# Loading the last 64 rows of w1 onto both partition halves, in a fused LayerNorm, scan and MLP kernel

## The chip, the cores and the metric

The kernel runs on one core of one Trainium2 chip. The metric is the device time of one launch in microseconds: 144.88 us, the median of three runs (144.66 to 145.1). A profile of one more execution gives every instruction's start and duration on the five engines: TensorE (PE, its weight loads as PEld), VectorE (DVE), ScalarE (ACT), GpSimd (POOL) and the queue engine SyncE (SP), which issues most DMAs.

## What is computed

All inputs are bf16; x has 2048 tokens of width D = 448, the MLP is F = 1792 wide. Cut to what matters:

```
xn = layernorm(x)                                   # over the 448 features
# branch A: diagonal complex scan over 2048 tokens
Bu[t] = B_bar @ xn[t];  h[t] = Lam_bar * h[t-1] + Bu[t]
s[t]  = 2 * Re(C @ h[t]) + xn[t] * Dskip
# branch B: LayerNorm again, then the MLP
y = layernorm(xn);  hdn = gelu(y @ w1 + b1);  g = silu(hdn @ w2 + b2)
out = x + s * g
```

## The kernel before

**Groups.** The tokens are worked in four groups g = 0 to 3 of 512, each made of two blocks b of 256 consecutive tokens. A block's even and odd tokens (`par` 0 and 1) stand side by side on 128 partitions, so each group has four tiles of 128 tokens.

**LayerNorm.** `ln_stats` and `ln_scale` give two scale and offset pairs per token: one for xn (branch A, tile `xn_sb`) and one for the doubly normalised y (branch B, tile `xn2_sb`). `ln_apply` (lines 444 to 453) writes 448 normalised columns into a row of 512. The last 64 columns are needed twice, since the rows are then transposed in pieces of 128 and every matmul uses 64 rows of the array at a time. For xn, `tail_twice` copies the last 64 columns behind themselves. For y, `ln_apply` writes two parts: columns 0 to 383, and then columns 320 to 447 (so the fourth piece of 128 begins with columns 320 to 383, which also stand in the third). A DMA transpose on SP (line 468) turns the rows into `xnT` or `xn2T`. The first block of group 0 is quicker: `first_stats` and `first_apply` (lines 384 to 422) work on each parity alone, and TensorE does the transposes of block 0 (line 415; pieces taken by `tcols`), which ACT and DVE then copy out of PSUM.

**The first MLP matmul, `mm1`.** `w1_sb` is 128 partitions by four row pieces by 1792 columns. Pieces 0 to 2 hold rows 0 to 383 of w1. Piece 3 holds rows 384 to 447 on partitions 64 to 127 (load `w1r`, line 348) and, on partitions 0 to 63, a copy of rows 320 to 383 that ACT or DVE makes from piece 2 after each load (line 342, keys `w1c_0` to `w1c_3`). `mm1_phase` (lines 655 to 675) computes a pair of F tiles (128 columns each, two PSUM banks) in two phases: the first does three row pieces, the second four, and within a step the two 64-row halves of the array work on two banks at once. After the second phase ACT does a Gelu per F tile into `gT`. For group 0 the two blocks are done apart (256 columns at a time), for the other groups 512 columns at a time. Every phase waits for its column chunk of w1 (`w1_0` to `w1_3`) and for `w1r`, a second phase for the copied rows too. w1 and w2 come in column chunks of 2, 4, 4 and 4 F tiles (`CH`, line 336).

**The rest.** `mm2` (and `mm2_tokens` for group 3) is the second MLP matmul, `bu_phase` is B_bar @ xn, `ssm` the scan on DVE, `yt` the output matmul of branch A. The tables for branch A (`parameters`, `tables`, `lb`, `cq`) are made on the chip from the small inputs; `b1_columns` turns b1 into columns by small matmuls from `brows`.

**The order of the work.** Every step is a task with the keys it reads and writes. `ORDER` (line 154) is a written-out list of task numbers; each engine and each DMA queue takes its own tasks in that order, and a task waits for the tasks whose keys it needs. `SECOND` lists the tasks that go to their second engine (ACT or DVE, POOL or DVE). SP takes, in this order: x block 0 even, odd, x block 1, `w1_0`, `w1r`, `w1_1`, `w1_2`, `w1_3`, the transpose of block 1, x blocks 2 and 3, four chunks of w2, the B matrices, and so on. The ACT queue takes seven small loads at the start: three vectors for branch A, b1 as three rows of 512 and one of 256, Dskip and b2. `dummies` are matmuls on constants whose result nobody reads.

Of the kernel before, what the change touches and what calls it, by code (L numbers as in the profile page):

```python
# [979 lines left out]
```

## Time and profile before

| what | value |
|---|---|
| time, median of three runs | 144.88 us (144.66 to 145.1) |
| the profiled execution | 145.18 us, of which the span from first to last instruction is 143.4 us |
| PE busy | 137.7 us, 96% of the span |
| DVE, ACT, POOL busy | 126.0, 105.9 and 24.7 us |
| DMA | 16.21 MB in 38530 packets |

A line of the timeline reads: start and duration in us, engine, code line, operation, tile written and tile read, shape, count, and in brackets the idle time ahead of it and what ended that. In a line of groups, the numbers behind the bar are busy us and the mean ns of one. L305 and L306 are the two arms of the helper `copy` (ACT and DVE), L77 and L78 the two forms of a DMA (transpose and plain), and L667 is every matmul of `mm1`. A line of DMA issues ends with the count, the KB of each and the median us from issue to landing. SPq and ACTq are the queues as issuers. The tables of windows give, for each stretch, the busy time of each engine, the granted TensorE clock, the share of busy DMA engines and the GB/s.

### The profile page before, as it was taken

The page shows a single profiled execution, that of the slowest core. Times are in us where ns is not written, and L with a number is a line of the kernel's source. Part 1 is how long each engine was busy: PE and PEld are TensorE (multiplying, and loading weights), DVE is VectorE, ACT ScalarE, POOL GpSimd, SP SyncE. Part 2 cuts the span into 40 slices and gives each one's busy share as a digit, 9 for nine tenths or more (in the row PEclk, how much of TensorE's full clock was granted, in tenths as well). Part 3 has the DMA queues.
Part 4 walks back from the last instruction along what each step waited for, and adds up shares of the span by engine and source line. Part 5 has one row for each costly group of instructions (what it writes and reads, how often), then busy time and mean ns, then how long its engine had stood idle before and what let it go on. Part 6 is the DMA issues. An engine that isn't in the chain of part 4 may idle for free.

```text
span 143.4 us, 3549 instructions
## 1 busy us (share of the span) xinstructions
PE 137.7 (96%) x1422; PEld 90.9 (63%) x1422; DVE 126.0 (88%) x275; ACT 105.9 (74%) x197; POOL 24.7 (17%) x83
## 2 busy tenths in 40 slices
PE   7999998999999989999999999999999999999991
PEld 7879953464455854566558844588777677665560
DVE  2979878998999679999999989993699998999994
ACT  3699959999996879879889359451777999928300
POOL 3389760256000700001000000200000001000000
DMA  4979997799997961010010745099830000003233
GB/s 101 240 238 249 311 331 184 152 245 184 199 189 148 151 134 35 0 32 0 7 32 0 61 108 110 0 199 193 160 126 9 0 5 0 18 5 69 49 119 128
DMA packets 38530, 16.21 MB, mean 113 GB/s; under 512 B 32937, under 2 KB 38066, under 8 KB 38514
## 3 DMA queue, kind: packets, MB, share of 16 engines
q1 hardware_dynamic: 38352, 15.92, 49.5%
q8 instruction: 11, 0.18, 0.5%
q10 hardware_dynamic: 162, 0.07, 0.2%
q14 instruction: 5, 0.04, 0.1%
HBM read 6.09 MB, written 1.84 MB: 55 GB/s over the span
## 4 chain that ended last, share of the span: by engine, by line
PE 63%; DMA 14%; DVE 13%; SPq 4%; ACT 1%; issue 1%; POOL 1%; DVEq 0%; ACTq 0%
PE psum L667 15%; PE psum L698 13%; PE psum L792 9%; PE psum L853 7%; DMA Bn<-in_A_B_re_dram 6%; PE psum L817 5%; DMA xnT<-xn_sb 5%; PE psum L816 5%; PE psum L382 3%; DMA Cr<-in_A_C_im_dram 3%; SPq L78 3%; DVE tmp L601 2%; DVE Bn L602 2%; PE psum L869 2%; PE psum L866 2%; DVE xn_sb L451 2%
## 5 line engine op out<-in xcount | busy, mean ns | idle before, releaser
L667 PE MATMUL psum<-xn2T,w_sb 64*128 64x512 bf16 (+1 forms) x490 | 46.5, 334 | 0.7 <-DMA w_sb<-in_B_w_dram 0.3
L673 ACT ACTIVATE gT<-psum,b1f 128x512 bf16<-128x512 f32 (+1 forms) x70 | 37.5, 607 | 4.5 <-PE psum L667 4.2
L667 PEld LDWEIGHTS psum<-xn2T,w_sb 64*128 64x128 bf16 x490 | 26.6, 108 | 13.9 <-ACT gT L673 1.0
L792 PE MATMUL psum<-gT,w_sb 128*128 128x512 bf16 x126 | 28.0, 379 | 0.7 <-ACT gT L673 0.6
L698 PE MATMUL psum<-xnT,BT 64*128 64x256 bf16 x392 | 25.0, 269 | 0.4 <-DVE u_sb L721 0.4
L698 PEld LDWEIGHTS psum<-xnT,BT 64*128 64x128 bf16 x392 | 19.2, 94 | 6.7 <-issue 1.0
L792 PEld LDWEIGHTS psum<-gT,w_sb 128*128 128x128 bf16 x126 | 11.9, 98 | 15.6 <-issue 1.5
L757 DVE TENSOR_TENSOR_SCAN s_w<-vs,dk 128x1048 f32<-128x1048 bf16 (+1 forms) x8 | 16.3, 2057 | 0.1
L452 ACT ACTIVATE xn_sb<-x_all,lnw 128x448 bf16<-128x448 bf16 (+2 forms) x16 | 10.0, 665 | 5.4 <-DMA xnT<-xn_sb 3.8
L853 PE MATMUL psum<-w_sb,gT 128*128 128x448 bf16 x56 | 10.9, 352 | 0.0
L474 ACT ACT_TABLE_LOAD x8 | 10.3, 1283 | 0.4
L305 ACT ACTIVATE ue<-psum 128x512 bf16<-128x512 f32 (+1 forms) x12 | 6.4, 562 | 5.3 <-PE psum L698 5.2
L451 DVE TENSOR_SCALAR xn_sb<-x_all,lnw 128x448 bf16<-128x448 bf16 (+2 forms) x24 | 8.0, 362 | 0.9 <-DVE lnw L441 0.5
L853 PEld LDWEIGHTS psum<-w_sb,gT 128*128 128x128 bf16 x56 | 5.5, 98 | 4.8 <-ACT psum L305 0.2
L305 ACT ACTIVATE vs<-s_w 64x258 bf16<-64x258 f32 (+2 forms) x11 | 6.5, 612 | 2.7 <-DVE s_w L757 2.6
L816 PE MATMUL psum<-hx,CZ 128*128 128x256 bf16 x63 | 8.4, 275 | 0.0
L817 PE MATMUL psum<-Bn,CQ 128*128 128x256 bf16 x63 | 8.2, 273 | 0.2 <-DVE Bn L777 0.2
L767 POOL TENSOR_TENSOR cur<-ang 128x8 f32<-128x8 f32 x2 | 0.4, 204 | 41.6 <-DVE ang L766 41.6
L798 ACT ACTIVATE g_sb<-psum,db 128x512 bf16<-128x512 f32 (+1 forms) x12 | 7.1, 629 | 0.6 <-PE psum L792 0.6
L369 DVE BATCH_NORM_STATS2 lnst<-x_all 128x6 f32<-128x448 bf16 x12 | 7.1, 613 | 0.4 <-DMA x_all<-in_A_x_dram 0.4
L816 PEld LDWEIGHTS psum<-hx,CZ 128*128 128x128 bf16 x63 | 5.9, 98 | 2.3 <-issue 0.4
L824 DVE TENSOR_TENSOR t<-psum,g_sb 128x512 bf16<-128x512 f32 (+1 forms) x12 | 7.1, 614 | 0.1
(161 smaller groups left out, 207.1 us busy)
## 6 DMA issues: line engine op xcount, KB each, us to landing
x_all<-in_A_x_dram SPq DMA_DIRECT2D x3, 448.0 KB, 4.3
w_sb<-in_B_w_dram SPq DMA_DIRECT2D x3, 448.0 KB, 5.3
out_dram<-Bn SPq DMA_DIRECT2D x6, 224.0 KB, 2.7
w_sb<-in_B_w_dram SPq DMA_DIRECT2D x3, 384.0 KB, 5.5
w_sb<-in_B_w_dram SPq DMA_DIRECT2D x2, 224.0 KB, 4.5
Bn<-in_A_B_im_dram SPq DMA_DIRECT2D x1, 336.0 KB, 6.5
Bn<-in_A_B_re_dram SPq DMA_DIRECT2D x1, 336.0 KB, 8.5
out_dram<-w_sb SPq DMA_DIRECT2D x3, 112.0 KB, 1.8
```

Of the source, the lines that this page charges most:

```text
L305: kb.either(("act", [lambda e, o=o, i=i: e.activation(o, i, ACT.Copy) for o, i in pairs]), ("dve", [lambda e, o=o, i=i: e.tensor_copy(o, i ...
L451: kb.either(("dve", [lambda e, o=o, i=i: e.tensor_scalar(o, i, rs, nb, op0=ALU.mult, op1=ALU.add) for o, i in parts]), ("act", [lambda e, ...
L452: ("act", [lambda e, o=o, i=i: e.activation(o, i, ACT.Identity, bias=nb, scale=rs) for o, i in parts]),
L474: kb.add("act", lambda e: e.preload_act_table_set(what), reads, writes, sem=name)
L667: return lambda e: e.matmul(dst(bk[k]), w1_sb[rows, d, fcol(2 * j + k)], rhs[rows, d], start=not second and n == 0, stop=second and n == 3)
L673: act(lambda e, k=k, fi=fi: e.activation(gT[:, gb, fi, cols], psum[:, bk[k], cols], ACT.Gelu_apprx_tanh, bias=b1f[:, fi:fi + 1]), ["b1f", ...
L698: fns.append(lambda e, rows=rows, bank=bank, m=m, o=o, n=n: e.matmul(psum[:, bank, c * NK:(c + 1) * NK].rearrange("p (b c) -> p b c", b=2) ...
L757: dve(lambda e, so=so, vi=vi, di=di: e.tensor_tensor_scan(so, vi, di, 0.0, ALU.add, ALU.mult), ["v", "vl", "vz", "dk", "dk01"] + ["v3"] * ...
L792: pe([lambda e, fi=fi: e.matmul(psum[:, bk, :], w2_sb[:, fi, 128 * j:128 * j + 128], gT[:, gb, fi, :], start=fi == 0, stop=fi == NF - 1) f ...
L816: pe([lambda e, k=k: e.matmul(par(psum[:, bk, :], 1), CZ[:, k, cols], halves(hx[:, hb, k, 1:NK + 1]), start=False, stop=k == 6, skip_group ...
L817: pe([lambda e, k=k: e.matmul(par(psum[:, bk, :], 0), CQ[:, k, cols], halves(hz[:, hb, k, :]), start=False, stop=k == 6, skip_group_check= ...
L853: pe([lambda e, fi=fi: e.matmul(P, gT[:, gb, fi, 128 * q:128 * q + 128], w2_sb[:, fi, :], start=False, stop=fi == NF - 1, skip_group_check ...
```

## The change

- `w1r` is now one DMA that writes all 128 partitions of piece 3: rows 384 to 447 of w1 twice, once onto each half. Its source pattern has a leading dimension of 2 with step 0. The copies of rows 320 to 383 (four tasks) are gone. Both halves of the array use piece n in step n, and a first phase no longer waits for `w1r`.
- The transposed y has the same form: `ln_apply` writes 448 columns in one part for both branches, and a new `tail` (the former `tail_twice`) doubles the last 64 columns, now for y too. TensorE's transposes of block 0 are three of 128 columns and two of 64 (`turn`).
- w1 and w2 come in chunks of 4, 4 and 6 F tiles.
- b1 is loaded as two rows of 512 and one of 768 and turned by ten small matmuls instead of six; Dskip and b2 are loaded from SP instead of ACT.
- In `parameters` one small operation is merged away, one ACT Exp over two columns becomes two, and one Abs may go to DVE. Four dummies are gone.
- `ORDER` and `SECOND` are new.

```diff
-            CH = ((0, 2), (2, 4), (6, 4), (10, 4))
+            CH = ((0, 4), (4, 4), (8, 6))
...
                 ld("sp", w1_sb[:, 0:3, a:a + w], dram_ap(B_w1, a, [[F, 128], [128 * F, 3], [1, w]]), [f"w1_{c}"])
-                copy([(w1_sb[0:64, 3, a:a + w], w1_sb[64:128, 2, a:a + w])], [f"w1_{c}"], [f"w1c_{c}"])
...
             ldx(1, 1)
+            ld("act", brows[0:2, 0:512], dram_ap(B_b1, 0, [[512, 2], [1, 512]]), ["br0"], ["br"])
+            ld("act", brows[2:3, :], dram_ap(B_b1, 1024, [[768, 1], [1, 768]]), ["br1"], ["br"])
             ldw1(0)
-            ld("sp", w1_sb[64:128, 3, :], dram_ap(B_w1, 384 * F, [[F, 64], [1, F]]), ["w1r"])
-            ld("act", brows[0:3, :], dram_ap(B_b1, 256, [[512, 3], [1, 512]]), ["br0"], ["br"])
-            ld("act", brows[3:4, 0:256], dram_ap(B_b1, 0, [[256, 1], [1, 256]]), ["br1"], ["br"])
-            for i, vec in enumerate((A_Dskip, B_b2)):
-                ld("act", drows[i:i + 1, :], dram_ap(vec, 0, [[D, 1], [1, D]]), [f"dbr{i}"])
+            ld("sp", w1_sb[:, 3, :], dram_ap(B_w1, 384 * F, [[0, 2], [F, 64], [1, F]]), ["w1r"])
             ldw1(1)
             ldw1(2)
-            ldw1(3)
+            for i, vec in enumerate((A_Dskip, B_b2)):
+                ld("sp", drows[i:i + 1, :], dram_ap(vec, 0, [[D, 1], [1, D]]), [f"dbr{i}"])
...
-            def tcols(b, par, d):
-                a = par * 512 + (0, 128, 256, 320)[d]
-                return xn2_sb[:, b, a:a + 128]
+            def turn(b, par, bank):
+                row, o = xn2_sb[:, b, par * 512:par * 512 + D], psh[:, bank, 0:512].rearrange("p (d c) -> p d c", d=4)
+                return [lambda e, d=d: e.transpose(o[:, d], row[:, 128 * d:128 * d + 128], ident[:, :]) for d in range(3)] \
+                    + [lambda e, h=h: e.transpose(o[h, 3], row[:, 384:D], ident[:, :]) for h in (slice(0, 64), slice(64, 128))]
...
+            def tail(rows, keys):
+                v = rows.rearrange("p b (r c) -> p (b r) c", r=2)
+                o, i = v[:, :, D:512], v[:, :, 384:D]
+                kb.either(("dve", lambda e: e.tensor_copy(o, i)), ("act", lambda e: e.activation(o, i, ACT.Copy)), keys, keys)
...
-                parts = [(row[:, 0:384], src[:, 0:384]), (row[:, 384:512], src[:, 320:D])] if which else [(row[:, 0:D], src)]
-                kb.either(("dve", [lambda e, o=o, i=i: e.tensor_scalar(o, i, rs, nb, op0=ALU.mult, op1=ALU.add) for o, i in parts]),
-                          ("act", [lambda e, o=o, i=i: e.activation(o, i, ACT.Identity, bias=nb, scale=rs) for o, i in parts]),
+                row = row[:, 0:D]
+                kb.either(("dve", lambda e: e.tensor_scalar(row, src, rs, nb, op0=ALU.mult, op1=ALU.add)),
+                          ("act", lambda e: e.activation(row, src, ACT.Identity, bias=nb, scale=rs)),
...
-                    rows, d = slice(64 * h, 64 * h + 64), (0, 1, 2 + h, 3 - h)[n]
+                    rows, d = slice(64 * h, 64 * h + 64), n
...
-                   xk2 + [f"w1_{c}", "w1r"] + ([f"w1c_{c}"] if second else []), [f"ps{bk[0]}", f"ps{bk[1]}"], split=True)
+                   xk2 + [f"w1_{c}"] + ["w1r"] * second, [f"ps{bk[0]}", f"ps{bk[1]}"], split=True)
...
-            dummies(4, ["st0"])
```

What the new order says, as far as the prediction speaks of it. SP: x block 0 even, odd, x block 1, `w1_0` (4 F tiles), `w1r`, `w1_1` (4), `w1_2` (6), the transpose of block 1, Dskip, x blocks 2 and 3, the first chunk of w2, b2, half of B, the other two chunks of w2, the other half of B, its two short ends, x blocks 4 and 5. PE: two first phases (both of chunk `w1_0`), two second phases (both of `w1_0`), and then chunk `w1_1`. DVE at the start: the stats of block 0, the apply of its even half, the first stats of block 1, two small steps, the apply of the odd half, a memset, the second stats of block 1 and two small steps, and then the copy of the odd half's transposes out of PSUM.

More of the change, by code (lines that the diff above doesn't have):

```diff
@@ L228, in bass_recurrent_scan__ssm_conv_s5__mixer_channel_mlp__prompt_kernel @@
         vrows = dk.bitcast(BF)[:, 1, 0:512]
-        brows = vrows[32:36, :]
+        brows = dk.bitcast(BF).rearrange("p i c -> p (i c)")[32:35, 2 * NS:2 * NS + 768]
         cw = SB("cw", [128, 32, 4], F32)
@@ L408, in first_apply @@
                     key = xk(0)[par:par + 1] if b == 0 else xk(1)
-                    parts = [(dst, src)] if b == 0 else [(xn2_sb[:, 1, par * 512:par * 512 + 384], src[:, 0:384]), (xn2_sb[:, 1, par * 512 + 384:par * 512 + 512], src[:, 320:D])]
-                    dve([lambda e, o=o, i=i, mean=mean, r1=r1: e.tensor_scalar(o, i, mean, r1, op0=ALU.subtract, op1=ALU.mult) for o, i in parts],
+                    dve(lambda e, dst=dst, src=src, mean=mean, r1=r1: e.tensor_scalar(dst, src, mean, r1, op0=ALU.subtract, op1=ALU.mult),
                         key + [f"r1{q}", f"mv0_{q}"], [f"xm{b}p{par}"])
@@ L414, in first_apply @@
                     bank, oap = 6 - par, xn2T[:, 0, b, par * 4:par * 4 + 4, :]
-                    pe([lambda e, d=d, par=par, bank=bank: e.transpose(psh[:, bank, d * 128:(d + 1) * 128], tcols(b, par, d), ident[:, :]) for d in range(4)],
+                    pe(turn(b, par, bank),
                        [f"xm{b}p{par}", "ident", f"xm{b}"], [f"ps{bank}"])
@@ L421, in first_apply @@
                 if b:
+                    tail(xn2_sb[:, 1:2], ["xm1p0", "xm1p1"])
                     kb.dma("sp", xn2T[:, 0, 1, :, :], xn2_sb[:, 1, :], reads=["xm1p0", "xm1p1", "xm1"], writes=["xmT1p0", "xmT1p1"], transpose=True)
@@ L449, in ln_apply @@
                 src = x_all[:, 2 * g + b, par, :]
-                parts = [(row[:, 0:384], src[:, 0:384]), (row[:, 384:512], src[:, 320:D])] if which else [(row[:, 0:D], src)]
-                kb.either(("dve", [lambda e, o=o, i=i: e.tensor_scalar(o, i, rs, nb, op0=ALU.mult, op1=ALU.add) for o, i in parts]),
-                          ("act", [lambda e, o=o, i=i: e.activation(o, i, ACT.Identity, bias=nb, scale=rs) for o, i in parts]),
+                row = row[:, 0:D]
+                kb.either(("dve", lambda e: e.tensor_scalar(row, src, rs, nb, op0=ALU.mult, op1=ALU.add)),
+                          ("act", lambda e: e.activation(row, src, ACT.Identity, bias=nb, scale=rs)),
                           [f"lnw{g % 2}_{b}"] + xk(2 * g + b), [key])
-            def tail_twice():
-                v = xn_sb[:].rearrange("p b (r c) -> p (b r) c", r=2)
-                o, i = v[:, :, D:512], v[:, :, 384:D]
-                kb.either(("dve", lambda e: e.tensor_copy(o, i)), ("act", lambda e: e.activation(o, i, ACT.Copy)), ["xn0", "xn1"], ["xn0", "xn1"])
             def ln(g, which):
@@ L463, in ln @@
                         ln_apply(g, b, par, which)
-                if not which:
-                    tail_twice()
                 src, dst = (xn_sb, xn2_sb)[which], (xnT, xn2T)[which]
+                tail(src[:], [("xn", "xm")[which] + str(b) for b in range(2)])
                 key, kT = ("xn", "xm")[which], ("xnT", "xmT")[which] + str(g % 2)
@@ L490, in parameters @@
                 small(lambda e: e.tensor_tensor(col(A1), col(DT), col(LRE), ALU.mult), ["cdt", "cp"], ["ca"])
-                small(lambda e: e.tensor_scalar(col(A1), col(A1), -DECAY_MAX, None, op0=ALU.max), ["ca"], ["ca"])
-                small(lambda e: e.tensor_scalar(col(NA1), col(A1), -1.0, None, op0=ALU.mult), ["ca"], ["cna"])
-                act(lambda e: e.activation(cw[:, R1:RI + 1, :], cw[:, A1:NA1 + 1, :], ACT.Exp), ["ca", "cna"], ["cr"])
+                small(lambda e: e.tensor_scalar(col(NA1), col(A1), -DECAY_MAX, -1.0, op0=ALU.max, op1=ALU.mult), ["ca"], ["cna"])
+                act([lambda e: e.activation(col(R1), col(NA1), ACT.Exp, scale=-1.0), lambda e: e.activation(col(RI), col(NA1), ACT.Exp)], ["cna"], ["cr"])
                 small(lambda e: e.tensor_tensor(ang[:, 0, 0, 0, :], col(DT), col(F2), ALU.mult), ["cdt", "f2"], ["f1"])
@@ L508, in parameters @@
                 small(wrap, ["f1", "f3", "f4"], ["f1"], True)
-                act(lambda e: e.activation(YB, YA, ACT.Abs), ["f1", "f2"], ["f1"])
+                kb.either(("act", lambda e: e.activation(YB, YA, ACT.Abs)), ("dve", lambda e: e.scalar_tensor_tensor(out=YB, in0=YA, scalar=-1.0, in1=YA, op0=ALU.mult, op1=ALU.max)),
+                          ["f1", "f2"], ["f1"])
                 small(sine, ["f1"], ["as", "ac"], True)
@@ L556, in b1_columns @@
             def b1_columns():
-                pe([lambda e, k=k: e.matmul(psum[:, 4, 2 + k:11 + k:4], brows[0:4, k:512:4], ident[32:36, 32:35], start=True, stop=True) for k in range(4)]
-                   + [lambda e, k=k: e.matmul(psum[:, 4, k:k + 1], brows[0:4, k:256:2], ident[32:36, 35:36], start=True, stop=True) for k in range(2)],
+                pe([lambda e, k=k: e.matmul(psum[:, 4, k:5 + k:4], brows[:, k:512:4], ident[32:35, 32:34], start=True, stop=True) for k in range(4)]
+                   + [lambda e, k=k: e.matmul(psum[:, 4, 8 + k:9 + k], brows[:, k:768:6], ident[32:35, 34:35], start=True, stop=True) for k in range(6)],
                    ["br", "br0", "br1", "ident"], ["ps4"])
@@ L853, in mm2_tokens @@
                 pe([lambda e, fi=fi: e.matmul(P, gT[:, gb, fi, 128 * q:128 * q + 128], w2_sb[:, fi, :], start=False, stop=fi == NF - 1, skip_group_check=True)
-                    for fi in range(NF)], [f"gT{gb}_{fi}_{h}" for fi in range(NF) for h in range(2)] + [f"w2_{c}" for c in range(4)], [f"ps{bk}"])
+                    for fi in range(NF)], [f"gT{gb}_{fi}_{h}" for fi in range(NF) for h in range(2)] + [f"w2_{c}" for c in range(len(CH))], [f"ps{bk}"])
                 act(lambda e: e.activation(g3[:, q, :], P, ACT.Silu), [f"ps{bk}", f"Ws{g}"], [f"g3_{q}"])
```

6 lines of the change are left out of this document (3 added, 3 removed), and 37 rows, old and new, of the table ORDER.

## The prediction

> **What bounds the kernel now.** The page first. TensorE is busy for nearly the whole span, so time is lost or won where it starts late, waits, or ends:
>
> ```profile
> span 143.4 us, 3549 instructions
> PE 137.7 (96%) x1422; PEld 90.9 (63%) x1422; DVE 126.0 (88%) x275; ACT 105.9 (74%) x197; POOL 24.7 (17%) x83
> ```
>
> Then the windows by stage: `mm1` of group 0 (7.3 to 18.8 us), `mm2` of group 0 and the tables, and the stretch to 51 us, where the loads and the making of the tables end.
>
> ```profile
> core 0: us, PE busy (x) PEld busy (x) DVE busy (x) ACT busy (x) POOL busy (x), PEclk, DMA share, GB/s
> 7.30:18.80 11.50, 11.30 (x199) 10.30 (x199) 10.15 (x41) 11.17 (x28) 9.68 (x31) 1.00 0.89 270
> 18.80:33.00 14.20, 13.61 (x99) 6.76 (x100) 12.81 (x47) 12.27 (x21) 5.45 (x20) 1.00 0.91 211
> 33.00:51.00 18.00, 17.31 (x190) 9.85 (x186) 16.17 (x40) 14.80 (x25) 4.44 (x8) 1.00 0.96 176
> ```
>
> TensorE idles 0.20, 0.59 and 0.69 us in the three, 1.5 us in all; the DMA engines are as full as TensorE. The timeline of TensorE shows what the idle time waits for:
>
> ```profile
> 0.83 2.93 PE L382 MATMUL psum<-const-bfloat16-1.0 128*128 128x128 bf16 x26 [0.83 <-PEq L965]
> 4.00 1.57 PE L382 MATMUL psum<-const-bfloat16-1.0 128*128 128x128 bf16 x13
> 6.38 0.64 PE L382 MATMUL psum<-const-bfloat16-1.0 128*128 128x128 bf16 x8
> 7.36 11.41 PE L667 MATMUL psum<-xn2T,w_sb 64*128 64x256 bf16 x196 [0.34 <-DMA w_sb<-in_B_w_dram]
> ...
> 23.20 5.77 PE L792 MATMUL psum<-gT,w_sb 128*128 128x512 bf16 x26 [0.59 <-ACT gT L673]
> 34.60 7.14 PE L667 MATMUL psum<-xn2T,w_sb 64*128 64x512 bf16 x64 [0.20 <-ACT gT L673]
> 51.00 1.81 PE L698 MATMUL psum<-xnT,BT 64*128 64x256 bf16 x30 [0.36 <-DVE u_sb L721]
> 52.74 6.22 PE L792 MATMUL psum<-gT,w_sb 128*128 128x512 bf16 x28
> ```
>
> `mm1` begins at 7.36 us, the moment a load of w1 lands. Which one, the DMA issues of the first 5 us tell, with the queue's issues in the timeline:
>
> ```profile
> q10 hardware_dynamic: 18, 0.01, 0.6%
> ...
> w_sb<-in_B_w_dram SPq DMA_DIRECT2D x3, 384.0 KB, 5.5
> ...
> w_sb<-in_B_w_dram SPq DMA_DIRECT2D x1, 224.0 KB, 4.6
> w_sb<-in_B_w_dram SPq DMA_DIRECT2D x1, 192.0 KB, 3.6
> ...
> dk<-in_B_b_dram ACTq DMA_DIRECT2D x1, 3.0 KB
> ```
>
> ```profile
> 2.18 2.73 SPq L78 DMA_DIRECT2D w_sb<-in_B_w_dram  x5
> ```
>
> Five issues from 2.18 us, some 0.55 us apart: `w1_0` (192 KB) lands at 2.18 + 3.6 = 5.8 us, `w1r` (224 KB) at about 2.7 + 4.6 = 7.3 us. So `w1r` opens `mm1`.
>
> **`w1r`: over how many DMA engines?** This decides the forecast. The ACT queue (q10) shows how a transfer is spread. In the first 5 us it moves seven loads, nine rows in all (six of one row, and b1 as three rows), in 18 packets: nine rows and nine more. Over the whole run:
>
> ```profile
> q10 hardware_dynamic: 162, 0.07, 0.2%
> ...
> out_dram<-w_sb ACTq DMA_DIRECT2D x1, 56.0 KB, 1.7
> ```
>
> The one store adds 162 - 18 = 144 packets: 128 rows and 16 more. Each engine that takes part thus ends with a small packet of its own: one for one row, three for three rows, 16 for 128 rows. The count follows the outermost dimension. In the new `w1r` the source's outermost dimension is 2 (the step-0 repeat), the destination's 128. I read it as two engines, one per copy; that the 128 rows decide is the first rival, since no transfer of this trace has two different counts.
>
> [...]
>
> The rate of one engine comes from seconds in which all are busy:
>
> ```profile
> 7.00:8.00 1.00, 0.60 (x9) 0.28 (x10) 0.85 (x6) 1.00 (x1) 0.83 (x4) 1.00 1.08 341
> 8.00:9.00 1.00, 1.00 (x20) 0.90 (x20) 0.53 (x4) 0.96 (x3) 0.83 (x3) 1.00 1.10 352
> ...
> 13.00:14.00 1.00, 1.00 (x23) 1.00 (x20) 1.00 (x3) 1.00 (x4) 0.92 (x3) 1.00 0.96 346
> ...
> 16.00:17.00 1.00, 1.00 (x24) 1.00 (x20) 1.00 (x4) 0.91 (x3) 0.75 (x4) 1.00 0.99 366
> ```
>
> 346/(16 x 0.96) = 22.5 and 366/(16 x 0.99) = 23.1 GB/s. Each of two engines moves 448 KB / 2 = 229,376 bytes: 9.9 to 10.2 us, somewhat less if two alone go faster than sixteen that share the memory. Estimate 9.5 us. On sixteen it is 1.2 us.
>
> **The sum.** (1) `w1_0` is now 384 KB; 192 KB more at 346 GB/s is 0.6 us, so it lands at 6.4 us. `w1r` follows it on its two engines. Its start is hidden in the latency of `w1_0`, up to 1 us of the 3.6, so it lands between 14.3 and 16.3 us; I take 14.9. (2) Before that TensorE can do the two first phases, 12 of the 196 matmuls. The old kernel had its twelfth at about 8.15 us (9 by 8.0, then 20 per us). So TensorE falls back by 14.9 - 8.15 = 6.75 us (6.15 to 8.15). When exactly `mm1` starts no longer matters.
>
> (3) After some 6 us of nothing TensorE may be slow. At the start 26 and 13 dummies of 128 columns ran at 113 and 121 ns, the later 8 at 80; a 512-wide matmul of the row at 52.74 takes 222 ns, 55 per 128 columns. That slow rate lasted for 4.5 us of work, so a return of it costs at most 2.25 us; at least nothing, since the longest wait after the start is 0.59 us and says nothing on pauses. A pause of 6 us is nearer to the start than to 0.59 us: I take 1.6.
>
> [...] The PEclk column reads 1.00 even over the slow dummies' stretch, so only durations will show it.
>
> (4) Behind a stalled TensorE its own later waits shrink: 1.5 us idle, and a stretch of `mm1` (11.41/196 = 58 ns against 7.14/64/2 = 56 for 256 columns, 0.5 us). ACT, 97% busy beside `mm1`, also loses two copies of w1 from its list:
>
> ```profile
> 5.79 0.41 ACT L305 ACTIVATE w_sb<-w_sb 64x256 bf16<-64x256 bf16 x1 [0.51 <-DMA w_sb<-in_B_w_dram]
> 8.50 0.63 ACT L305 ACTIVATE w_sb<-w_sb 64x512 bf16<-64x512 bf16 x1
> ```
>
> That is another 1.0 us. Bounds -0.5 to -3.0; I take -1.9, the waits and the stretch, because its Gelus come after the stall too.
>
> (5) What is late next: `w1_1` and `w1_2` queue behind `w1r` on the two engines (24 and 36 KB each, 1.1 and 1.6 us), landing near 16.0 and 17.6 us. The two second phases (16 matmuls, 0.9 us, or 1.8 slow) and then four phases (28, 1.6 us) reach them at 15.8 to 18: covered within 0.3 us. Then the transpose and x blocks 2 and 3 follow, landing near 20 us. DVE waited for those at 15.21 us:
>
> ```profile
> 15.21 1.68 DVE L369 BATCH_NORM_STATS2 lnst<-x_all 128x6 f32<-128x448 bf16 x3 [0.39 <-DMA x_all<-in_A_x_dram]
> ```
>
> So DVE falls back by under 5 us, less than TensorE. The chain of waits shows the next load that matters:
>
> ```profile
> 14.98 8.51 DMA Bn<-in_A_B_re_dram
> ...
> 51.00 1.81 PE psum L698 x30
> ```
>
> It landed at 23.5 us. The two engines then carry, each, transposes, x, three chunks of w2 and two of B, some 8 us from 17.6, so it lands near 26: 2 to 3 us late. TensorE stays the last.
>
> **The other edits** cost nothing on that path or little:
>
> ```profile
> L451 DVE TENSOR_SCALAR xn_sb<-x_all,lnw 128x448 bf16<-128x448 bf16 x10 | 3.9, 389 | 0.4 <-DMA xnT<-xn_sb 0.4
> L451 DVE TENSOR_SCALAR xn_sb<-x_all,lnw 128x384 bf16<-128x384 bf16 x7 | 2.6, 376 | 0.6 <-DVE lnw L441 0.5
> L451 DVE TENSOR_SCALAR xn_sb<-x_all,lnw 128x128 bf16<-128x128 bf16 x7 | 2.2, 309 | 0.0
> L458 DVE COPY xn_sb<-xn_sb 128x256 bf16<-128x256 bf16 x3 | 0.6, 215 | 0.0
> ```
>
> An apply in one part saves 376 + 309 - 389 = 0.3 us, four per transpose, less 0.2 for the tail: 1 us of DVE or ACT per group. The transpose now waits for all four and the tail. TensorE is busy meanwhile, so I take 0; without that cover it is 1 us per group, either way. Two more transposes and four more b1 columns (about 0.1 us each) and four dummies fewer fall into the time before `w1r`. The merged small step, the split Exp, Abs, and the two loads moved to SP (some 0.55 us of issue each, behind the backlog) do too, or lie behind busy engines. The new order after 51 us moves pieces of like size: 0, bounds -0.3 to +0.4.
>
> Sum against the profiled execution's own 145.18 us: +6.75 +1.6 -1.9 = +6.45, 151.6 us. That execution is 0.3 above the median, 144.88, so the forecast is 151.3. Bounds: 145.18 - 0.3 + 6.15 + 0 - 3.0 - 0.3 = 147.7 and + 8.15 + 2.25 - 0.5 + 0.4 = 155.2.
>
> **Rivals.** *Sixteen engines (the other side).* If the 128 rows decide, `w1r` lands at 7.3 us plus (192 + 224 KB)/346 GB/s = 1.2 us, at 8.5. The second phases need it two first phases after the start, so nothing waits, and that holds from eight engines up (448 KB in 2.5 us, 8.9 us). Then the start of `mm1` counts:
>
> ```profile
> 5.22 0.40 DVE L410 TENSOR_SCALAR xn_sb<-x_all,lnmv,lnw 128x448 bf16<-128x448 bf16 x1 [0.18 <-ACT lnw L393]
> 5.54 0.62 DVE L389 BATCH_NORM_STATS2 lnst<-x_all 128x6 f32<-128x448 bf16 x1
> 6.21 0.43 DVE L306 COPY xn2T<-psum 128x512 bf16<-128x512 bf16 x1
> ```
>
> The new order puts one stats (0.62) and two small steps ahead of that apply, and another stats and small steps ahead of that copy, which then ends near 7.7 us instead of 6.64: `mm1` starts about 0.35 late. In return ACT is 1.0 us lighter and the waits for Gelus (0.59, 0.20) go. Net -0.45: 144.4 us. For it: destinations decide in every transfer seen, as far as the trace can tell. Against: the source is walked too.
>
> *The stall is taken back.* Two engines, no slow rate, and all 3.0 us absorbed: +3.75, 148.6 us. For: ACT and DVE are as full as TensorE and get ahead. Against: they depend on its results.
>
> *The loads follow in full.* All later loads come 9.5 - 1.2 = 8.3 us late, and with them the chain from the B load to 51.0 us, since the DMA share is 0.89 to 0.96 up to there: +8.3, 153.2 us. Against: the fourteen other engines are free and the queue had holes.
>
> **Chances and range.** Forecast 0.53 (149.5 to 153.5), taken back 0.15, loads follow 0.12, sixteen engines 0.15, something else 0.05. Range 147.3 to 155.0: it leaves out the sixteen engines and a little more. Runs of this kernel differ by 0.3%, which is what a measurement tells from no change. Sixteen engines give faster 0.09, the same 0.04, slower 0.02; the rest is slower: 0.87.
>
> **What would show it.** `w1r` (448 KB) some 12 us from issue to landing, TensorE idle from about 9 to 15 us on a DMA of `w_sb`, DMA at a few tens of GB/s there, dummies' rates in the first matmuls after it, the last `mm1` of group 0 near 26 us instead of 18.8. Wrong, if `w1r` lands by 9 us, or if the distance at 51 us is far from 6.

## The result, and the profile after

The changed kernel takes 156.19 us (median of 4 runs, 155.55 to 156.44), the kernel before 144.99 in the same comparison: 1.0764 times as long, interval 1.0722 to 1.0807. The forecast, 151.3 us, had the direction and the main cause, and was 4.9 us short; its range ended at 155.0. The profiled execution took 156.2 us, with a span of 154.5. Of the kernels below, e1 has one slow execution among its six and e13 four, which raise their medians and ranges.

First the page, then TensorE's timeline (columns as before):

```profile
span 154.5 us, 3539 instructions
PE 138.9 (90%) x1420; PEld 91.9 (59%) x1424; DVE 125.9 (82%) x294; ACT 103.3 (67%) x192; POOL 18.1 (12%) x60
```

```profile
7.18 0.85 PE L664 MATMUL psum<-xn2T,w_sb 64*128 64x256 bf16 x12 [0.26 <-DVE xn2T L305]
15.54 12.82 PE L664 MATMUL psum<-xn2T,w_sb 64*128 64x256 bf16 x184 [7.52 <-DMA w_sb<-in_B_w_dram]
28.80 9.01 PE L789 MATMUL psum<-gT,w_sb 128*128 128x512 bf16 x41 [0.16 <-issue]
...
59.55 1.81 PE L695 MATMUL psum<-xnT,BT 64*128 64x256 bf16 x30 [0.73 <-DVE u_sb L718]
...
80.52 0.50 PE L695 MATMUL psum<-xnT,BT 64*128 64x256 bf16 x6 [0.77 <-DVE u_sb L718]
...
149.07 0.83 PE L866 MATMUL psum<-CQ,Bn 128*128 128x224 bf16 x7
```

TensorE does 12 matmuls of `mm1`, stands for 7.52 us on a load of `w_sb`, and needs 12.82 us for the other 184; the first run of `mm1` ends at 28.36 us, before at 18.77 (7.36 + 11.41). The windows show the stall, the granted clock behind it and an almost empty set of DMA engines:

```profile
core 0: us, PE busy (x) PEld busy (x) DVE busy (x) ACT busy (x) POOL busy (x), PEclk, DMA share, GB/s
7.30:18.80 11.50, 3.98 (x44) 2.77 (x43) 6.90 (x38) 2.19 (x5) 6.99 (x23) 0.64 1.06 106
18.80:33.00 14.20, 14.04 (x181) 10.87 (x179) 10.08 (x42) 12.34 (x29) 0.47 (x3) 0.93 0.69 235
33.00:51.00 18.00, 18.00 (x167) 10.06 (x167) 12.81 (x37) 15.58 (x25) 0.00 (x0) 1.00 1.01 177
```

270 GB/s have become 106 in the first window. Its DMA share of 1.06 misleads: the one microsecond from 10 to 11 reads 8.62. In the stall behind it the share is 0.12 to 0.13, which is two of sixteen engines:

```profile
11.00:12.00 1.00, 0.00 (x0) 0.00 (x0) 0.93 (x8) 0.00 (x0) 0.83 (x3) 0.50 0.12 50
12.00:13.00 1.00, 0.00 (x0) 0.00 (x0) 1.00 (x11) 0.00 (x0) 0.60 (x4) 0.50 0.13 54
13.00:14.00 1.00, 0.00 (x0) 0.00 (x0) 0.78 (x5) 0.00 (x0) 0.35 (x2) 0.50 0.13 54
```

The chain of waits that ended last gives the load's time from issue to landing, and how the chain goes on: over `mm1`, ACT's Gelus and the work on ACT's list behind them to VectorE.

```profile
2.68 12.82 DMA w_sb<-in_B_w_dram
15.50 0.05 issue
15.54 12.40 PE psum L664 x176
27.97 0.91 ACT gT L670 x2
...
36.36 0.62 ACT tmp L597
36.98 0.03 issue
37.01 0.75 DVE Bn L599
```

SP's timeline shows what happened to its queue:

```profile
2.20 2.96 SPq L78 DMA_DIRECT2D w_sb<-in_B_w_dram  x4
8.90 5.40 SPq L77 DMA_TRANSPOSE xn2T<-xn_sb  x1
14.35 0.44 SPq L78 DMA_DIRECT2D dk<-in_A_Dskip_dram  x1
14.84 0.39 SPq L78 DMA_DIRECT2D x_all<-in_A_x_dram  x1
```

`w1r` is issued at 2.68 us and lands at 15.50. In the trace's packet records its 128 rows run from 4.91 to 15.04 us, and between 9.7 and 15.5 us only two small packets (4 bytes, one per engine by the prediction's reading) appear, at 14.53 and 15.03. SP itself stood for 5.40 us in the issue of one transpose. The loads behind were late, and VectorE waited 7.18 us for x blocks 2 and 3:

```profile
22.43 0.63 DVE L366 BATCH_NORM_STATS2 lnst<-x_all 128x6 f32<-128x448 bf16 x1 [7.18 <-DMA x_all<-in_A_x_dram]
```

Before, that wait ended at 15.21 us. Last the end, SP's stores of the kernel before (first fence) and after (second):

```profile
139.74 1.79 SPq L78 DMA_DIRECT2D out_dram<-w_sb  x4
```

```profile
148.06 0.34 SPq L78 DMA_DIRECT2D out_dram<-Bn  x1
148.96 2.61 SPq L78 DMA_DIRECT2D out_dram<-w_sb  x3
151.61 0.45 SPq L78 DMA_DIRECT2D out_dram<-Bn  x1
152.11 0.45 SPq L78 DMA_DIRECT2D out_dram<-w_sb  x1
```

The last matmul ends at 149.90 us (before 140.44), 9.46 later; from there to the end of the span it is 4.56 us instead of 3.01 (the traces' spans are 154.46 and 143.45 us). So 1.55 us of the loss arise behind the last matmul.

### The profile page after: what moved, and what is told of

The parts are those of the page before. It is cut to its first block, busy times and chain, and to the rows that moved or that the text cites. A ratio compares the mean times of both kernels' runs of the same rounds, so it can differ in the third digit from the quotient of the medians.

```text
span 154.5 us, 3539 instructions
## 1 busy us (share of the span) xinstructions
PE 138.9 (90%) x1420; PEld 91.9 (59%) x1424; DVE 125.9 (82%) x294; ACT 103.3 (67%) x192; POOL 18.1 (12%) x60
## 4 chain that ended last, share of the span: by engine, by line
PE 39%; DVE 32%; DMA 14%; ACT 6%; POOL 3%; issue 2%; SPq 1%; DVEq 0%; ACTq 0%
PE psum L664 15%; DMA w_sb<-in_B_w_dram 8%; PE psum L695 7%; PE psum L850 7%; DVE s_w L754 5%; PE psum L813 3%; PE psum L814 3%; DMA x_all<-in_A_x_dram 3%; DVE lnst L366 3%; DVE tmp L598 3%; DMA Cr<-in_A_C_re_dram 3%; DVE CQ L599 3%; DVE vs L305 2%; DVE Bn L599 2%; PE psum L863 2%; POOL lnw L436 2%
## 5 line engine op out<-in xcount | busy, mean ns | idle before, releaser
L664 PE MATMUL psum<-xn2T,w_sb 64*128 64x512 bf16 (+1 forms) x490 | 48.4, 349 | 7.8 <-DMA w_sb<-in_B_w_dram 7.5
L664 PEld LDWEIGHTS psum<-xn2T,w_sb 64*128 64x128 bf16 x490 | 28.7, 119 | 21.1 <-DMA w_sb<-in_B_w_dram 7.8
L789 PE MATMUL psum<-gT,w_sb 128*128 128x512 bf16 x122 | 27.0, 379 | 0.5 <-issue 0.5
L695 PEld LDWEIGHTS psum<-xnT,BT 64*128 64x128 bf16 x392 | 18.6, 94 | 8.6 <-DVE u_sb L718 2.0
L754 DVE TENSOR_TENSOR_SCAN s_w<-vs,dk 128x786 f32<-128x786 bf16 (+1 forms) x8 | 16.2, 2053 | 0.0
L304 ACT ACTIVATE ue<-psum 128x512 bf16<-128x512 f32 (+1 forms) x14 | 7.3, 552 | 6.3 <-PE psum L695 6.3
L850 PE MATMUL psum<-w_sb,gT 128*128 128x448 bf16 x56 | 10.9, 353 | 0.0
L454 DVE TENSOR_SCALAR xn_sb<-x_all,lnw 128x448 bf16<-128x448 bf16 x20 | 7.5, 391 | 3.8 <-DMA xnT<-xn_sb 2.5
L810 ACT ACTIVATE psum<-xnT,db 128x512 f32<-128x512 bf16 (+1 forms) x15 | 8.8, 603 | 2.0 <-DVE u_sb L305 1.9
L304 ACT ACTIVATE vs<-s_w 64x258 bf16<-64x258 f32 (+2 forms) x10 | 5.2, 528 | 5.5 <-DVE s_w L754 5.4
L304 ACT ACTIVATE u_sb<-psum 128x256 bf16<-128x256 f32 (+1 forms) x13 | 5.5, 465 | 2.4 <-PE psum L695 2.4
```

The costliest lines, as they stand in the source:

```text
L304: kb.either(("act", [lambda e, o=o, i=i: e.activation(o, i, ACT.Copy) for o, i in pairs]), ("dve", [lambda e, o=o, i=i: e.tensor_copy(o, i ...
L664: return lambda e: e.matmul(dst(bk[k]), w1_sb[rows, d, fcol(2 * j + k)], rhs[rows, d], start=not second and n == 0, stop=second and n == 3)
L695: fns.append(lambda e, rows=rows, bank=bank, m=m, o=o, n=n: e.matmul(psum[:, bank, c * NK:(c + 1) * NK].rearrange("p (b c) -> p b c", b=2) ...
L754: dve(lambda e, so=so, vi=vi, di=di: e.tensor_tensor_scan(so, vi, di, 0.0, ALU.add, ALU.mult), ["v", "vl", "vz", "dk", "dk01"] + ["v3"] * ...
L789: pe([lambda e, fi=fi: e.matmul(psum[:, bk, :], w2_sb[:, fi, 128 * j:128 * j + 128], gT[:, gb, fi, :], start=fi == 0, stop=fi == NF - 1) f ...
L810: kb.either(("act", [lambda e, o=o, x=x, d=d: e.activation(v(o), x, ACT.Copy, scale=d) for o, x, d in seeds]), ("dve", [lambda e, o=o, x=x ...
```

## The experiments

One table serves all. Times in the first three columns are from the profiled executions: the end of the first `mm1` run, the start of VectorE's first statistics on x blocks 2 and 3, the end of the last matmul. "Tail" is from there to the end of the span. The last column is the median of the timed runs. The other columns are one execution each, and executions of one kernel differ (the kernel before took 143.8 to 145.9 us in all but one of those that were timed beside these), so a few tenths of a microsecond between two rows prove nothing.

| kernel | mm1 ends | x 2, 3 | last matmul | tail | us |
|---|---|---|---|---|---|
| before | 18.77 | 15.21 | 140.44 | 3.01 | 144.99 |
| changed | 28.36 | 22.43 | 149.90 | 4.56 | 156.19 |
| e1 split | 18.51 | 15.60 | 140.69 | 4.54 | 147.76 |
| e7 lead 64 | 19.58 | 15.42 | 141.21 | 4.54 | 147.13 |
| e8 before, lead 2 | 26.46 | 19.46 | 147.20 | 3.01 | 151.09 |
| e9 useless load | 20.05 | 26.78 | 151.75 | 4.59 | 157.95 |
| e3 ACT's queue | 32.29 | 27.29 | 154.04 | 4.54 | 161.89 |
| e10 ACT's queue, last | 30.45 | 21.89 | 152.60 | 4.55 | 158.72 |
| e2 dummies | 27.45 | 21.48 | 150.33 | 4.54 | 156.15 |
| e11 x 6, 7 early | 28.12 | 23.82 | 149.12 | 4.55 | 155.21 |
| e12 e11 + dummies | 27.55 | 21.40 | 148.31 | 4.54 | 155.04 |
| e14 e11 + w1_1 first | 28.54 | 21.98 | 149.63 | 4.54 | 155.92 |
| e15 e14 + dummies | 28.05 | 20.91 | 148.98 | 4.56 | 155.18 |
| e5 split, wait moved | 20.32 | 15.71 | 141.81 | 3.55 | 147.25 |
| e6 e5 + x 6, 7 early | 19.89 | 15.56 | 141.12 | 3.55 | 146.60 |
| e13 e6, tiles 2444 | 19.85 | 15.16 | 140.53 | 3.56 | 148.36 |
| e16 e6 + store moved | 20.14 | 15.43 | 141.08 | 3.01 | 145.57 |

The numbers suggest a simple rule. From the end of `mm1` to the last matmul it takes 120.7 to 122.9 us in every kernel but e9 (131.7), whatever was done to the loads and the clock; and from the statistics on x 2 and 3 it is never less than 125.0 us (before 125.2, split 125.1, e9 125.0). I read this as two chains side by side, of which the later one sets the end. The rule is good to about 2 us only.

### The load as two loads

```diff
-            ld("sp", w1_sb[:, 3, :], dram_ap(B_w1, 384 * F, [[0, 2], [F, 64], [1, F]]), ["w1r"])
+            for h in (0, 64):
+                ld("sp", w1_sb[h:h + 64, 3, :], dram_ap(B_w1, 384 * F, [[F, 64], [1, F]]), [f"w1r{h}"])
```

> The changed kernel, but w1r is two loads of 64 rows each (224 KB, outermost count 64 on both sides), one behind the other, instead of one load with the repeat as its outermost dimension; all else as changed, computation whole. Two-engine theory (the one load runs on two DMA engines and holds TensorE, SP and with them DVE; the rest of the change is small): each half lands 4 to 7 us after its issue, TensorE has no wait above 1 us in mm1, and the time is 143.5 to 146.5 us (the kernel before: 145.0). Rival A (the step-0 repeat or 448 KB of traffic costs as such): w1r's halves are late too, over 150 us. Rival B (the new order itself costs the 1.6 us seen in the tail and about 1 us on VectorE): no stall but 146.5 to 148.5 us.

147.76 us (146.98 to 149.31), 1.0219 of before (1.0154 to 1.0283). TensorE's and SP's lines:

```profile
7.22 11.29 PE L665 MATMUL psum<-xn2T,w_sb 64*128 64x256 bf16 x196 [0.26 <-DVE xn2T L305]
...
50.35 1.81 PE L696 MATMUL psum<-xnT,BT 64*128 64x256 bf16 x30 [0.46 <-DVE u_sb L719]
...
71.33 0.50 PE L696 MATMUL psum<-xnT,BT 64*128 64x256 bf16 x6 [0.78 <-DVE u_sb L719]
```

```profile
8.94 1.33 SPq L77 DMA_TRANSPOSE xn2T<-xn_sb  x1
```

No stall, and the transpose is issued in 1.33 us. The form of this one load makes 8.4 of the 11.2 us. The time isn't that of the two-engine theory (143.5 to 146.5) but rival B's: the rest of the change costs 2.7 us by itself (1.8 in the profiled executions, 146.98 against 145.18), and 1.53 of it are the tail, 4.54 against 3.01. The rest lies behind 51 us: TensorE's group of 30 `BT` matmuls starts at 50.35 us, 0.65 ahead of the kernel before (51.00), but the last matmul ends 0.25 later, with a wait of 0.78 us at 71.33 us that the kernel before doesn't have.

### The outermost count, or the step of 0?

Kernel e7 keeps one load with the repeat, but inside (rows land in other partitions, so that the products over rows 384 to 447 differ); e8 is the kernel before, whose `w1r` gets an outermost count of 2 without any repeat (here too the rows land in another order).

```diff
-[[0, 2], [F, 64], [1, F]]
+[[F, 64], [0, 2], [1, F]]      # e7, in the changed kernel
...
-[[F, 64], [1, F]]
+[[F, 2], [2 * F, 32], [1, F]]  # e8, in the kernel before
```

> The changed kernel with the source pattern of w1r as 64 rows, each given twice (step 0 inside, outermost count 64): the same one load, the same 448 KB read and written, the same destination. Each row lands in two neighbouring partitions instead of 64 apart, so the products over rows 384 to 447 are not those of the reference; every instruction and its shapes are the same. Theory that the outermost count of the source decides over how many engines a load is spread: w1r lands within 7 us of its issue, no stall above 1 us, 146 to 149 us, as with two loads (147.8). Rival (a step of 0, reading the same rows twice, makes the load slow): the stall stays, over 152 us.

> The kernel before with the source pattern of its w1r (64 rows, 224 KB, into the lower row half) as 2 groups of every second row: outermost count 2, no step 0, nothing read twice, the same bytes. The 64 rows land in another order, so the products over rows 384 to 447 are not those of the reference; every instruction and its shapes are the same. Theory (an outermost count of 2 means two DMA engines whatever the step): w1r lands some 7 us after its issue instead of 4.6 (112 KB by each engine at 22 to 23 GB/s are 5 us), mm1 opens 2 to 4 us later and the loads behind it follow: 147 to 149.5 us against 144.8. Rival (only a step of 0 confines a load): within 0.5 us of 144.8.

e7: 147.13 us (146.65 to 147.51), as with two loads (147.76) and as expected; the step of 0 cost nothing extra. e8: 151.09 us (149.83 to 151.95), 1.0408 of before (1.0324 to 1.0492), and this is its TensorE:

```profile
12.81 13.65 PE L667 MATMUL psum<-xn2T,w_sb 64*128 64x256 bf16 x196 [6.08 <-DMA w_sb<-in_B_w_dram]
```

The outermost count decided here, not the repeat: TensorE's longest wait in `mm1` or ahead of it was 7.52 us with a count of 2 and the repeat, 6.08 with 2 and no repeat (e8), 0.39 with 64 and the repeat (e7). (No run gives `w1r` a count between 2 and 64: a kernel with 16, e4, gave no time.) e8's loss was larger than expected: its 64 rows ran from 5.04 to 12.30 us in the packet records, on two engines 227 ns for each of an engine's 32 rows, where the changed kernel's took (15.04 - 4.91)/64 = 158. The records show when they were slow: a row took mostly 200 to 290 ns between 7.0 and 10.1 us, with other loads under way, and 140 ns from 10.9 us on. The changed kernel's rows, too, took 140 ns from 9.6 us on.

### What the held queue does by itself

The split kernel gets a useless load of the slow form (w1's last rows into the place of x blocks 6 and 7, loaded properly later), behind everything that `mm1` needs and ahead of x 2 and 3:

```diff
+            ld("sp", x_all[:, 6:8, :, :], dram_ap(B_w1, 384 * F, [[0, 2], [F, 64], [1, F]]), ["x6", "x7"])
```

> The split kernel (147.8 us) with one more load that nothing needs: w1's last 64 rows twice, outermost count 2 with step 0, into the place of x blocks 6 and 7, which are loaded properly long after. It is issued on SP's queue behind the transpose of x block 1 and ahead of x blocks 2 and 3, so that all inputs of the first mm1 run are ahead of it and TensorE's mm1 isn't touched, while x, B and w2 queue behind it as they do behind w1r in the changed kernel. Theory that TensorE's own wait for w1r makes the loss and the late loads behind it are mostly hidden: mm1 ends at 18.5 us as in the split kernel, VectorE waits some 6 to 7 us for x blocks 2 and 3, the time rises by no more than 3 us: 148 to 151. Rival (VectorE's late start on x and B alone carries the loss; TensorE's wait lies within it): the time rises by 6 to 9 us, 154 to 157.

157.95 us (157.65 to 158.37), more than either theory said. `mm1` wasn't hurt, but the list behind it was:

```profile
12.19 7.86 PE L666 MATMUL psum<-xn2T,w_sb 64*128 64x256 bf16 x140 [0.89 <-DMA w_sb<-in_B_w_dram]
27.04 0.21 PE L562 MATMUL psum<-ident,dk 2*128 2x2 bf16 x3 [6.99 <-issue]
```

```profile
26.78 0.63 DVE L368 BATCH_NORM_STATS2 lnst<-x_all 128x6 f32<-128x448 bf16 x1 [11.51 <-DMA x_all<-in_A_x_dram]
```

So a load behind which others queue can cost this much without holding `mm1`, and 0.9 KB were enough to stop TensorE: L562 reads the rows of Dskip and b2, which the change moved from ACT's queue to SP's (the profile names no releaser for the 6.99 us; that tile is what the instruction reads). It doesn't separate VectorE from TensorE, as it was meant to. It gives the lowest value for the second chain: x 2 and 3 at 26.78, last matmul 125.0 us later; which of the late loads sets that end isn't separated, since TensorE itself stood for one of them. In the changed kernel that chain would end at 22.43 + 125.0 = 147.4 us, 2.5 us ahead of the 149.90 that was seen. By this reading `mm1` leads there, as it does in the profile's own chain of waits, and the late loads lie behind it.

### The load on the other queue

```diff
-            ld("sp", w1_sb[:, 3, :], dram_ap(B_w1, 384 * F, [[0, 2], [F, 64], [1, F]]), ["w1r"])
+            ld("act", w1_sb[:, 3, :], dram_ap(B_w1, 384 * F, [[0, 2], [F, 64], [1, F]]), ["w1r"])
```

In e10 its place in the order is also behind the second load of b1.

> The changed kernel with the one w1r load (outermost count 2) issued by ACT's queue instead of SP's; nothing is left out. It separates TensorE's wait for w1r from the backlog of the loads behind it on SP's queue. Theory that most of the loss is TensorE's wait alone: w1r lands when it did (13 to 16 us), TensorE waits 6 to 8 us, x blocks 2 and 3 and B are issued some 4 to 5 us earlier, and the time falls by no more than 1 us: 155 to 156.5. Rival (the loads behind it on SP's queue carry several us of the loss, through VectorE): TensorE's wait in mm1 is as long, but VectorE's 8.2 us wait for x shrinks under 4 us and the time falls to 152 to 154.

> The changed kernel with the one w1r load (outermost count 2) issued by ACT's queue behind both loads of b1, instead of by SP's queue (in the earlier run on ACT's queue it stood ahead of a b1 load that TensorE's list needed, which hid the question). It separates what w1r does to the loads that follow on its own queue from TensorE's wait for it. Theory from the run with the useless load (the loads queued behind w1r carry most of the loss): x blocks 2 and 3 land 3 us or more before the 22.4 us of the changed kernel, TensorE's wait is as long, and the time falls by 1 to 4 us: 152 to 155. Rival (TensorE's wait carries it all the same): within 0.7 us of 156.2.

e3: 161.89 us (160.34 to 162.04), outside both ranges. A load of b1 stood behind `w1r` and came at 18 us; TensorE's list stopped at b1:

```profile
18.28 0.27 PE L554 MATMUL psum<-ident,dk 3*128 3x2 bf16 x4 [12.51 <-DMA dk<-in_B_b_dram]
```

e10: 158.72 us (158.51 to 160.6), against both theories. On the other queue `w1r` lands later, and the other loads not much earlier:

```profile
18.37 12.08 PE L664 MATMUL psum<-xn2T,w_sb 64*128 64x256 bf16 x184 [10.23 <-DMA w_sb<-in_B_w_dram]
```

x 2 and 3 come 0.54 us earlier than in the changed kernel (and SP's last load of this stretch, of x 4 and 5, is issued at 21.42 us instead of 23.36), `mm1` ends 2.09 later, the last matmul 2.70 later. Where the two move apart, the end goes with `mm1`: the first chain is the one in charge.

### The slow clock

120 dummies behind the 12 matmuls keep TensorE busy in the stall. e2 is the changed kernel with them; e11 has the load of x 6 and 7 early, e12 both; e14 is e11 with `w1_1` ahead of `w1r`, e15 that with 140 dummies.

```diff
                     mm1_phase(0, b, j, p, False)
+                    if b == 0 and j == 1:
+                        dummies(120, bank=7)
...
-SP order: ... w1_0 w1r w1_1 ...   x4x5 <six transposes> x6x7
+SP order: ... w1_0 w1r w1_1 ...   x4x5 x6x7    # e11, e12
+SP order: ... w1_0 w1_1 w1r ...   x4x5 x6x7    # e14, e15
```

> The changed kernel with 120 dummy matmuls of 128 columns (into bank 7, which nothing uses then) on TensorE's list right behind the 12 matmuls that precede the stall, so that TensorE is busy for some 6.6 us of the 7.5 us that it waits for w1r; nothing is left out. Theory that a slow clock after the pause costs time on the path: the granted clock stays near 1.0 in 7.3 to 18.8 us instead of 0.64, the 184 matmuls behind the stall take about 11.0 us instead of 12.8, and the time falls by 1.3 to 2.2 us, to 154.0 to 154.9. Rival (the chain is held by the late loads and by VectorE behind them, so TensorE's clock is not what sets the end): the clock is restored but the time stays within 0.5 us of 156.2.

> The changed kernel with one move: the load of x blocks 6 and 7 on SP's queue right behind that of blocks 4 and 5, as in the kernel before, instead of behind six transposes (issued at 51.90 us). Nothing is left out. Theory: VectorE's wait of 1.0 us for it at 56.5 us goes and 0.3 to 1.0 us of it reach the end: 155.2 to 155.9 (changed kernel: 156.2). Rival (other late work holds VectorE there): no difference.

> The run before with the 120 dummies in TensorE's wait for w1r. It asks whether the slow clock's price (0.9 us at the end of the first mm1 run, by the kernel with dummies alone, which lost it again where VectorE waited 2.0 us for x blocks 6 and 7) reaches the end once that load is early. Theory: 0.6 to 1.0 us under the run before. Rival (the late loads of x and B hold VectorE and the chain runs over them, so TensorE's clock costs nothing): within 0.3 us of the run before.

> The changed kernel with the early load of x blocks 6 and 7 (155.2 us) and w1_1 issued ahead of w1r instead of behind it; nothing is left out. w1r then lands about 1.1 us later (384 KB more ahead of it), TensorE waits some 8.6 us, and its 184 matmuls run without a further wait but at the slow clock: mm1 ends near 29 us, 155.7 to 156.7. It is the first of a pair.

> The run before with 140 dummies in TensorE's wait. Theory that the slow clock has a price that only the wait for w1_1 had hidden: the 184 matmuls take 10.3 to 10.8 us instead of 12 to 12.8, mm1 ends 1.3 to 2.3 us earlier than in the run before, and 1.0 to 2.0 us of it reach the end. Rival (after the stall the loads of x, B and w2 behind w1r hold the other engines, so an earlier end of mm1 is worth nothing): mm1 ends earlier but the time is within 0.4 us of the run before.

156.15, 155.21, 155.04, 155.92 and 155.18 us. e11 and e14 lie where they were expected (though TensorE waited 6.60 us in e14, not 8.6), e2 and e12 where their rivals put them, e15 between the two. TensorE's lines of e12, then of e14 and of e15:

```profile
15.64 1.42 PE L664 MATMUL psum<-xn2T,w_sb 64*128 64x256 bf16 x20 [0.42 <-DMA w_sb<-in_B_w_dram]
18.34 9.21 PE L664 MATMUL psum<-xn2T,w_sb 64*128 64x256 bf16 x164 [1.28 <-issue]
```

```profile
16.20 12.34 PE L664 MATMUL psum<-xn2T,w_sb 64*128 64x256 bf16 x184 [6.60 <-DMA w_sb<-in_B_w_dram]
```

```profile
17.73 10.32 PE L664 MATMUL psum<-xn2T,w_sb 64*128 64x256 bf16 x184 [1.11 <-issue]
```

The dummies do restore the clock: 10.32 us for 184 matmuls, against 12.05 in e11, 12.34 in e14 and 12.82 in the changed kernel. The slow clock is worth 1.7 to 2.5 us on TensorE. The trace's record of the granted clock agrees: it stands at 0.50 until 20.87 us in the changed kernel, 5.3 us after TensorE resumes, and until 19.75 us in e11, 3.7 us after. The runs can't show that much at the end, because every kernel with dummies gets a new idle time of 1.1 to 1.3 us. I had taken that for a wait for `w1_1`; e15 has `w1_1` first and keeps it, so that was wrong, and what it is stays open (the profile names no releaser). As far as single executions show it, what is left does arrive: `mm1` ends 0.57 and 0.49 us earlier in the two pairs, the last matmul 0.81 and 0.65, the medians 0.17 and 0.74 (with ranges that overlap). In e2 alone the 0.91 us of `mm1` were lost again where VectorE waited 2.0 us for x 6 and 7. That load's place costs the changed kernel some 0.5 to 1.0 us (149.90 to 149.12 at the last matmul, of which 0.24 is an earlier end of `mm1`; 156.19 to 155.21 in time).

### The tail and the rest

```diff
-        settle = [t for t in order if t.eng == "sp"][-4]
+        settle = [t for t in order if t.eng == "sp"][-6]        # e5, in e1
...
-SP order: ... x4x5 <six transposes> x6x7                        # e6, in e5
+SP order: ... x4x5 x6x7
...
-SP order: ... out20 out300 out322 out310 out21 out330           # e16, in e6
+SP order: ... out21 out20 out300 out322 out310 out330
...
-            CH = ((0, 4), (4, 4), (8, 6))                       # e13, in e6
+            CH = ((0, 2), (2, 4), (6, 4), (10, 4))
```

(At its task `settle` SP waits for all transfers issued so far. e13 also makes b1's columns from four rows, as before.)

> The split kernel (two loads of 64 rows for w1r), in which SP waits for all transfers so far before its sixth last task instead of its fourth last. In the split kernel's trace the fourth last task of SP stands right behind two stores that were issued 0.9 and 0.5 us before, so SP seems to wait there for their landing: its last store is issued at 142.89 us though its data are ready at 141.5. Theory (this wait is the tail's 1.5 us): the last store is issued by 141.8, the time falls by 0.9 to 1.3 us against the split kernel's 147.8, to 146.4 to 146.9. Rival (SP needs 0.45 to 0.5 us for each of six stores and would be late anyway): under 0.4 us.

> The kernel of the run before with the load of x blocks 6 and 7 moved on SP's queue from behind six transposes (issued at 42.92 us) to right behind that of blocks 4 and 5 (about 16.7 us), where the kernel before had it (26 us). Theory (VectorE waits for it and carries the chain from 41 to 101 us): VectorE's wait of 0.5 us at 47.33 us goes, the last matmul ends 0.3 to 0.8 us earlier, 145.6 to 146.4 us. Rival (VectorE has other work to wait with, and the early load delays the transposes): within 0.3 us of the run before.

> The kernel with two loads for w1r, SP's early wait moved and the early load of x blocks 6 and 7 (146.6 us), with w1 and w2 in tiles of 2, 4, 4, 4 as in the kernel before instead of 4, 4, 6, and b1's columns made from four rows as there. It asks what the larger tiles cost: in the run with 4, 4, 6 TensorE waits 0.9 us at 12 us for w1_1, behind 832 KB of w1. Theory: that wait shrinks to under 0.4 us, the time falls by 0.4 to 0.9 us, to 145.7 to 146.2. Rival (what is left of the loss lies in the stores' order at the end and in VectorE's list): within 0.3 us of 146.6.

> The kernel with two loads for w1r, SP's wait moved and the early load of x blocks 6 and 7 (146.6 us), in which the store of block 5 stands on SP's queue ahead of the store of block 4, not between the last stores (it was issued 0.48 us before the very last one). Theory: the last store is issued 0.4 to 0.5 us earlier after the last matmul, the time falls by 0.3 to 0.5 us to 146.1 to 146.3. Rival (the last store waits for VectorE's last sum anyway): within 0.2 us of 146.6.

e5: 147.25 us (146.4 to 147.8), 0.5 less than the split kernel instead of 0.9 to 1.3, though its tail is 0.99 us shorter; in its profile `mm1` ended 1.8 us later than in e1's. e6: 146.60 (145.98 to 147.19), its last matmul 0.69 earlier than in e5, as expected, its time 0.2 above the range. e16: 145.57 (145.11 to 147.24), the tail again 0.54 shorter, as expected, the time below the range. SP's stores in e5, then in e16:

```profile
140.87 1.30 SPq L78 DMA_DIRECT2D out_dram<-w_sb  x3
142.22 0.43 SPq L78 DMA_DIRECT2D out_dram<-Bn  x1
142.69 0.46 SPq L78 DMA_DIRECT2D out_dram<-w_sb  x1
```

```profile
138.55 1.02 SPq L78 DMA_DIRECT2D out_dram<-Bn  x2
140.15 2.03 SPq L78 DMA_DIRECT2D out_dram<-w_sb  x4
```

The three stores that took 2.61 us take 1.30 once SP no longer waits among them for the stores it has just issued, and with block 5's store out of the way the tail is 3.01 us, as before: the split kernel's 1.53 us are all accounted for. e13: 148.36 us (145.87 to 148.75). Its six executions fall apart, four at 148.3 to 148.75 us and two at 145.87 and 147.1, and in the profiled one TensorE waits 1.57 us for a load of w1 up to 9.25 us, where e6's waits 0.94 up to 12.03. What the larger tiles cost isn't settled.

e16, the best version, is still 1.007 of before (1.0036 to 1.0104). Its last matmul ends 0.64 us later than before, with `mm1` 1.37 later: TensorE waits there for 1.12 us at 12.3 us, as in e5, e6 and e9 (0.89 to 1.29 us) and not in e1. The profile puts it down to a load of w1, in e5 to a Gelu; what it is wasn't settled.

## Why the prediction was too low

By its own steps:

- **(1) Two engines: right** (a share of 0.12 to 0.13 in the stall). 12.82 us from issue to landing. The rows took 10.1 us, which is the 9.9 to 10.2 of its own division; the "somewhat less" that made it 9.5 held only once the other loads had gone (140 ns a row then, 158 on average). TensorE resumed at 15.54, not 14.9.
- **(2) Twelve matmuls, then the stall: right,** to the count. The distance (how far TensorE is behind the kernel before) when it ends is 15.54 - 8.15 = 7.39 us, forecast 6.75: 0.64 short.
- **(3) A slow rate after the pause: right in kind.** At the old pace the 184 matmuls would be 184 x 11.41/196 = 10.71 us; they took 12.82. The distance grows by 2.20 us, to 9.59 at the end of `mm1`, where 1.6 was taken: short by 0.60. That PEclk would not show it was wrong for this execution (0.64 in the window). It reads 1.00 where the trace has no record of the clock: the trace of the kernel before has none at all, e14's begins only at 20.48 us, behind its slow matmuls.
- **(4) "Behind a stalled TensorE its own later waits shrink", -1.9: this step failed in its size.** The waits for Gelus went, but the one for VectorE at 51 us, which was to go too, grew: 0.73 us at 59.55 instead of 0.36. At that point the distance is 59.55 - 51.00 = 8.55 us: 1.04 of the 9.59 was taken back, not 1.9. In e8, the old order behind a stall, it was 1.24 (7.69 to 6.45); from the split to the changed kernel, one order with and without the stall, 0.65 (9.85 to 9.20). That ACT and DVE get ahead during the stall was the thought; but the chain of waits runs over ACT's work behind the late `mm1` to VectorE, and VectorE's inputs came late on the same queue. By the forecast's own sign (wrong, "if the distance at 51 us is far from 6") 8.55 counts against it.
- **(5) "TensorE stays the last": right,** by 2.5 us if the second chain is 125.0 us long, though VectorE fell back by 7.2 us and not by "under 5". SP being held in its issues for 5.4 us was not in the forecast.
- **(6) "The new order after 51 us moves pieces of like size: 0, bounds -0.3 to +0.4": this step failed, and it is the largest miss, +2.46 us.** Behind 59.55 us TensorE loses another 0.91 (8.55 to 9.46), most of it in the wait of 0.77 at 80.52 us for VectorE's `u_sb`; then come the 1.55 of the tail. Neither needs the stall: the split kernel has the same 0.90 (from 0.65 ahead to 0.25 behind), the same wait (0.78 at 71.33 us) and a tail that is 1.53 longer. e5 and e16 trace the tail to SP's wait among the last stores and to the place of block 5's store. What in VectorE's new list makes the wait for `u_sb` wasn't isolated (e11 and e16 still have 0.62). I looked at the size of the pieces and not at the waits between them; SP's last six stores, the task numbers and the `settle` line were there to be read.

In sum, from the forecast's 151.6 to the 156.2 of the profiled execution: 0.64 + 0.60 + 0.86 + 0.91 + 1.55 = 4.6 us. So two engines and the stall were right, and more than half of what was missing comes from the other edits, which had been put at nothing. The rival "the loads follow in full" came nearer in time (153.2), but for a reason that isn't the main one: the runs put `mm1` ahead of the loads in this kernel.
